# Moving DRAM copies earlier, operand sums later and weight sums apart in a one-core attention and MLP kernel

## The chip, the cores and the metric

The kernel runs on one core of a Trainium2 chip. The metric is the device time of one execution in microseconds (us). The engines are TensorE (PE, with its weight loads PEld), VectorE (DVE), ScalarE (ACT), GpSimd (POOL) and SyncE (SP), which here only issues DMAs. ACT issues DMAs too.

## The reference

A block with adaptive layer norm: attention on the last 512 keys of a cache, then a gated MLP. All data are 32-bit floats; S = 2048 tokens, D = 576, 32 query heads and 16 key heads of 128, F = 4608.

```python
sa, ca, ga, sb, cb, gb = (silu(c) @ w_mod).reshape(6, 576)
h = layernorm(x) * (1 + ca) + sa
p = softmax(q(h) @ k[-512:].T * 128 ** -0.5)         # per head
x = x + ga * ((p @ v[-512:]) @ wo)
h = layernorm(x) * (1 + cb) + sb
gate, up = h @ W_gate, h @ W_up
x = x + gb * ((gate * (gate > 0) * up) @ W_down)
```

## The kernel before, in words

Every product is made of 32-bit parts: an operand is split into `hi` (a rounded copy, made by ACT) and `lo` (the rest, a subtraction on POOL), and PE multiplies hi by hi, hi by lo and lo by hi.

Attention is 128 units, u = 0 to 127: one query head with 512 tokens. The instructions of PE, DVE, ACT and POOL are issued in the order in which the program is written. `step(name, t, fn)` puts extra work at the place t, in tenths of a unit: t = 705 is in the middle of unit 70. Each unit has one transposing reduction on DVE at line 474, by which units can be counted. SyncE's order is made by a scheduler, which may put a DMA that waits for nothing earlier than its step.

The extra work in the units:
- weights for the next heads are loaded (`rwA` for queries, `rkv` for keys and values, `roga` for the output), split and partly stored again;
- the MLP's gate and up weights are copied within DRAM into another layout, `wlay` and `wlay0` (`lay_steps`: 20 first copies, 68 big ones of shape 2x128x256, 64 small ones of shape 8 or 9x32x128), all on SyncE's queue;
- `w_later` makes the seven weight operands of feature pair 0 from `wlay0`, with loads (`wa_P`, `wb_P`), sums on POOL and stores;
- from H = 1070 on (unit 107), the second layer norm and the operands of the MLP's first token half.

The MLP uses a scheme of seven products (P1, P6, P2, P7, P5, P4, P3, in this order) in place of eight for a 2x2 block of tokens and features. One feature pair m is 256 features; m = 0 to 17 works on the first half of the tokens, m = 18 to 35 on the second. Seven token operands (B11, B21, B22, T1 to T4) stay in SBUF through a half. They are made from four quarters of h, `h0[j, k, t]` (t = 0, 1, 2 are the thirds along D), in place: `t3` overwrites (1,1) by (1,1) - (0,1), `t2` then adds (0,0), `t1` and `t4` come last. `h0_hi` makes `hi` on ACT, `h0_cut` makes `lo` on POOL, and most are stored and loaded again (`h_back`).

For m = 1 to 17 the weight operands are made while m - 1 is computed: four raw tiles `wr` (00, 01, 10, 11) are loaded from `wlay`, DVE makes four sums of them in place, and `w_split` splits each of the seven operands. For m = 18 to 35 they come back from DRAM. The down product of m - 1 is eight pieces `md`, spread over the products of m; each piece uses the one bank of `psW`, which is free again when DVE has added it to `acc` (line 594). A piece needs `hhi` and `hlo`, the split of the gated result, which `evac` makes: three DVE instructions (L969 to L971), `hi` on ACT, `lo` on POOL. `wd_prep` loads the two down-weight tiles of an m, multiplies them by the gate row on DVE (`rogb`, L221) and splits them. DVE's L967, once in each m, counts the m's.

Of the kernel before, what the change touches and what calls it, by code (L numbers as in the profile page):

```python
# [33 lines left out]
def kernel(  # L34
# [667 lines left out]
    def w_split(n, raw):  # L702
        w = w_tile(n)
        nc.scalar.copy(w[:, :, 0:3, :], raw)
# [8 lines left out]
    loads = []  # L713

    def w_prep(n):
        w_prep1(n)
        while loads:
            w_load(*loads.pop(0))

    def w_prep1(n):  # L720
        m, s = divmod(n, 7)
        if m >= NB:
            return
        s = order(m)[s]
# [7 lines left out]
        if s == "P1":  # L732
            s1 = wraw[m, "s1"] = pp.tile([P, 2, 3, P], F32, tag="hi", name=f"ws1_{m}")
            nc.vector.tensor_tensor(flat(s1), flat(r[1, 0]), flat(r[1, 1]), op=ALU.add)  # L734
        if s == "P1":
            w_split(n, r[0, 0])
        elif s == "P6":
            nc.vector.tensor_tensor(flat(r[1, 0]), flat(r[0, 0]), flat(r[1, 0]), op=ALU.subtract)  # L738
            nc.vector.tensor_tensor(flat(r[0, 0]), flat(wraw[m, "s1"]), flat(r[0, 0]), op=ALU.subtract)  # L739
            w_split(n, r[0, 0])  # L740
        elif s == "P2":
            w_split(n, r[0, 1])
        elif s == "P7":
            nc.vector.tensor_tensor(flat(r[0, 1]), flat(r[0, 1]), flat(r[0, 0]), op=ALU.subtract)
            w_split(n, r[1, 0])
        elif s == "P5":
            w_split(n, wraw[m, "s1"])
        elif s == "P4":
            w_split(n, r[1, 1])
        else:  # L750
            w_split(n, r[0, 1])

# [70 lines left out]
    def h0_here(s):  # L823
        for t in range(3):
            h0_hi(s, H0_CUT[s], t)
        hs = hop[0, s] = [hy0[s, t] for t in range(3)]
        for t in (0, 1, 2):
            a = h0[(*H0_CUT[s], t)]
            if t < 2:
                hs.append(hp.tile([P, 512], F32R, tag="hT", name=f"hz0_{s}_{t}"))  # L830
                nc.gpsimd.tensor_sub(hs[-1], a, hs[t].bitcast(F32))
            else:
                nc.gpsimd.tensor_sub(hs[2][64:96], a[64:96], hs[2][64:96].bitcast(F32))

    def h0_cut(s, x, t):
        a, n = h0[(*x, t)], 96 if t == 2 else P
        hi = hy0[s, t]
        if t < 2:
            lo = hp.tile([P, 512], F32R, tag="hT", name=f"hz0_{s}_{t}")
            nc.gpsimd.tensor_sub(lo, a, hi.bitcast(F32))  # L840
            stores.append((hkeep[0, s, 3 + t], lo))
        else:
            nc.gpsimd.tensor_sub(hi[64:96], a[64:96], hi[64:96].bitcast(F32))
# [364 lines left out]
    step("m5.l", 936, m5_back)  # L1208
    step("gb", 949, setd(mods, "gb", lambda: gate_row(5)))

    step("T.ohi2", e, o_hi, NU - 2)
    step("T.olo2", e, o_lo, NU - 2)
    for k, lay in enumerate(lay_steps()):
        for i, ab in enumerate(lay):
            step("lay", (480, 600)[k] + 3.4 * i, lambda ab=ab: nc.sync.dma_start(*ab))
    mextra = {}

    def mat(m, s, fn, *args):
        mextra.setdefault((m, s), []).append((fn,))

    for m in range(NB):
        for f in range(2):
            for k, fn in enumerate(wd_prep(m, f)):
                mat(m, (k, 3 + (k > 0))[f] if m else 2 * f + k, fn)
    for i in range(4):
        m = 2 + 2 * i
        for at_, fn in zip(((m - 1, 5), (m, 0), (m, 1), (m, 5)), ln_half(2 + i // 2, i % 2)):
            mat(*at_, fn)
# [7 lines left out]
    LEAD = 3  # L1236
    def mlp_slots():
        todo = []
        for m in range(NB):
            md = [lambda k=k, qt=qt: md_piece(m - 1, k, qt) for k in range(2) for qt in range(4)] if m else []  # L1240
            for i, s in enumerate(order(m)):
                flush_stores()
                if s not in ("P2", "P3"):
                    new_pair(m, s)
                else:
                    pair[m, s], kind[m, s] = (x[m, {"P2": "P1", "P3": "P5"}[s]] for x in (pair, kind))
                prod(m, s, 7 * m + i, 0)
# [52 lines left out]
    for s in ("P1", "P2", "P4", "P7", "P5", "P6", "P3"):  # L1300
        for xx in range(2):
            for fn in w_later(s, xx, (xp, "xm", 640)):
                step("w.l", t, fn)
                t = after(t + 5)
            step("w.e", t + 3, flush_stores)
            t = after(t + 5)
    assert t < 930, t
    for key, t, at_ in [(("l", 0, 0), 2, 96), (("l", 1, 0), 2, 96), (("l", 1, 1), 2, 122), (("l", 0, 1), 2, 122),
# [162 lines left out]
```

## Time and profile before

| | |
|---|---|
| median of 3 runs | 3068.1 us (3067.82 to 3068.15) |
| profiled execution | 3069.0 us, of which span 3067.2 us |
| busy, share of the span | PE 95%, DVE 68%, ACT 45%, POOL 61% |
| granted clock, mean | 0.981 |
| data moved | 427.24 MB, mean 139 GB/s |

"Profiled execution" is one run under the profiler; the span goes from its first to its last instruction, and all times in rows are from the start of that span. In rows of stretches, the columns after the length are the busy us of each engine with the number of instructions, the clock that PE was granted, the mean busy share of the 16 DMA engines, and the GB/s moved. A row "A <- B: 10.0, 4, 3.0" says that A's engine stood idle 10.0 us in all before A until B was done, 4 times, at most 3.0 us.

### The profile page before, as it was taken

How to read it: one execution, taken by the hardware profiler on the slowest of the kernel's cores; microseconds unless marked ns; L12 is line 12 of the kernel's file. 1: busy time of each engine (PE TensorE's matmuls, PEld its weight loads, DVE VectorE, ACT ScalarE, POOL GpSimd, SP SyncE). 2: the span in 40 equal slices, each digit the busy share in tenths (PEclk: the TensorE clock that was granted, in tenths of full speed). 3: DMA queues.
4: the chain of work that ended last, by engine and by line, in shares of the span. 5: the costliest groups of instructions: out<-in, count | busy, mean ns of one | idle time of the engine just before them, and what ended most of it. 6: DMA issues, size and time to landing. Idle time of an engine off the chain costs nothing. (4 is left out here: it accounts for less than half of the span.)

```text
span 3067.2 us, 41142 instructions
## 1 busy us (share of the span) xinstructions
PE 2914.7 (95%) x15406; PEld 2536.8 (83%) x15406; DVE 2092.0 (68%) x2909; ACT 1368.0 (45%) x1869; POOL 1874.8 (61%) x1315
## 2 busy tenths in 40 slices
PE   6799999999999779999988999999999999999999
PEld 5688888888888668888877788888888888888888
DVE  7878788888887558777877566666666544444444
ACT  5466676666666446666645433333333111111110
POOL 5578888888888568767776566667787311111111
PEclk9899999999999889999999999999999999999999
DMA  4011122112222223432244355667777944444543
GB/s 144 21 50 57 45 76 69 64 53 76 88 84 85 85 80 129 156 98 90 68 146 143 104 202 215 240 243 263 272 259 253 344 172 160 159 161 167 175 161 115
DMA packets 168679, 427.24 MB, mean 139 GB/s; under 512 B 15584, under 2 KB 62432, under 8 KB 168480
## 3 DMA queue, kind: packets, MB, share of 16 engines
q1 hardware_dynamic: 132848, 294.08, 29.4%
q10 hardware_dynamic: 35632, 130.53, 11.1%
q8 instruction: 122, 2.00, 0.3%
q14 instruction: 77, 0.63, 0.1%
HBM read 279.42 MB, written 173.44 MB: 148 GB/s over the span
## 5 line engine op out<-in xcount | busy, mean ns | idle before, releaser
L538 POOL TENSOR_TENSOR lo<-p,hi 128x1024 fp32r<-128x1024 f32 x256 | 612.9, 2416 | 1.1 <-ACT hi L518 0.8
L547 POOL TENSOR_TENSOR ks<-ks,p 128x512 f32<-128x512 f32 x256 | 339.6, 1326 | 295.7 <-ACT p L531 236.7
L594 DVE TENSOR_TENSOR acc<-md,acc 128x576 f32<-128x576 f32 x288 | 217.9, 756 | 437.8 <-PE md L583 437.8
L583 PE MATMUL md<-wogb,hhi 128*128 128x288 f32 x2304 | 472.1, 297 | 21.0 <-DVE acc L594 21.0
L583 PEld LDWEIGHTS md<-wogb,hhi 128*128 128x128 f32 x2304 | 386.6, 189 | 49.4 <-DVE acc L594 27.8
L459 DVE TRANSPOSE_TENSOR_REDUCE t<-s 128x32 f32<-128x1024 f32 x256 | 316.7, 1244 | 155.2 <-PE s L456 143.8
L946 PE MATMUL gu<-hop_T,wop 128*128 128x512 f32 (+1 forms) x1512 | 380.7, 395 | 3.0 <-DVE rb L564 3.0
L946 PE MATMUL gu<-hop_B,wop 128*128 128x512 f32 (+1 forms) x1512 | 379.1, 394 | 2.2 <-DMA wop<-wk_P 2.0
L583 PE MATMUL md<-wogb,hlo 128*128 128x288 f32 x1152 | 342.7, 297 | 12.0 <-POOL hlo L962 12.0
L382 PE MATMUL qps<-hTa,wA 128*128 128x512 f32 x1288 | 314.5, 396 | 15.1 <-ACT lfa L364 7.8
L946 PEld LDWEIGHTS gu<-hop_B,wop 128*128 128x128 f32 (+1 forms) x1512 | 279.1, 189 | 57.4 <-DMA wop<-wk_P 2.4
L962 POOL TENSOR_TENSOR hlo<-r,hhi 128x512 fp32r<-128x512 f32 x72 | 101.5, 1410 | 366.6 <-issue 244.7
L946 PEld LDWEIGHTS gu<-hop_T,wop 128*128 128x128 f32 (+1 forms) x1512 | 279.7, 190 | 55.0 <-DVE rb L564 3.1
L583 PE MATMUL wo<-woga,ohi 128*128 128x288 f32 x1472 | 311.6, 305 | 7.1 <-ACT wo L616 5.2
L382 PEld LDWEIGHTS qps<-hTa,wA 128*128 128x128 f32 x1288 | 245.8, 191 | 68.6 <-ACT lfa L364 8.2
L529 DVE TENSOR_TENSOR p<-s,mb 128x1024 f32<-128x1024 f32 x246 | 290.2, 1218 | 4.2
L518 ACT CAST hi<-p 128x1024 fp32r<-128x1024 f32 x256 | 269.1, 1051 | 7.2
L531 ACT ACTIVATE p<-p 128x1024 f32<-128x1024 f32 x246 | 259.8, 1056 | 7.9 <-DVE p L529 5.9
L583 PEld LDWEIGHTS wo<-woga,ohi 128*128 128x128 f32 x1472 | 243.1, 192 | 15.3 <-ACT wo L616 5.6
L583 PEld LDWEIGHTS md<-wogb,hlo 128*128 128x128 f32 x1152 | 217.7, 189 | 15.0 <-POOL hlo L962 15.0
L583 PE MATMUL wo<-woga,olo 128*128 128x288 f32 x736 | 220.2, 299 | 8.3 <-POOL olo L572 8.1
L434 ACT ACTIVATE qhi<-qps 128x512 fp32r<-128x512 f32 x128 | 76.4, 597 | 333.9 <-PE qps L382 333.6
(207 smaller groups left out, 6000.2 us busy)
## 6 DMA issues: line engine op xcount, KB each, us to landing
wop<-wk_P SPq DMA_DIRECT2D x133, 640.0 KB
wk_P<-wop ACTq DMA_DIRECT2D x119, 640.0 KB
wr<-wlay SPq DMA_DIRECT2D x68, 384.0 KB
dk<-wogb ACTq DMA_DIRECT2D x36, 576.0 KB
wogb<-dk SPq DMA_DIRECT2D x36, 576.0 KB
againq<-akq SPq DMA_DIRECT2D x18, 640.0 KB
rogb<-wd SPq DMA_DIRECT2D x36, 288.0 KB
rwA<-wq SPq DMA_DIRECT2D x32, 320.0 KB
```

Of the source, the lines that this page charges most:

```text
L382: return [lambda i=i, a=a, b=b: nc.tensor.matmul(ps, a, b, start=(i == 0), stop=(i == n - 1)) for i, (a, b) in enumerate(ops)]
L434: nc.scalar.activation(qhi[u], qst[u][0], AF.Copy, bias=0.0, scale=SCALE)
L459: nc.vector.tensor_reduce(t4[u][:, 2 * h:2 * h + 2, :].rearrange("p k b -> p (k b)"), t.rearrange("p k (b j) -> p (k b) j", j=32), axis=AX ...
L518: nc.scalar.copy(hi_[u, h], pt[u, h])
L529: nc.vector.tensor_tensor(p, t, bc[u][:, None, :].to_broadcast([P, 2, 512]), op=ALU.subtract)
L531: nc.scalar.activation(p, p, AF.Exp, bias=0.0, scale=1.0)
L538: nc.gpsimd.tensor_sub(lo_[u, h], pt[u, h], hi_[u, h].bitcast(F32))
L547: nc.gpsimd.tensor_tensor(ks_[u], ks_[u], p[:, j, :], op=ALU.add)
L583: nc.tensor.matmul(ps[:, half, :H2], a[:, sl], w[b][:, cs], start=(n == 0 and seed is None), stop=(n == 5), skip_group_check=seed is not None)
L594: nc.vector.tensor_tensor(av, ps[:, :, :H2], av, op=ALU.add)
L946: nc.tensor.matmul(ps, a, c, start=s not in ("P2", "P3") and i == 0, stop=i == len(ops) - 1, skip_group_check=True)
L962: nc.gpsimd.tensor_sub(lo, r, hi.bitcast(F32))
```

## The change

1. The copies. First and other copies form one list that starts at step 400 with 3.5 between steps; before, the first ones started at 480 and the others at 600, 3.4 apart. `w_later` has 8 in place of 5 between its steps and more places to choose from; the saved row m5 comes back at 1046 and not at 936.
2. The token operands. Steps of `h0_comb` and `h0_cut` come later, so that a sum that overwrites a tile stands about ten steps behind the split that reads it. The split of the third tile (t = 2) moves from POOL to DVE. T2 stays in SBUF: it is neither stored nor loaded again.
3. The MLP's weights. The four sums per m are other ones (S3, S2, S1, S4 in this order) and stand in P4 and P3 of m - 1 and in P6 and P2 of m, one in each; before, P4 had one, P3 two, P6 the fourth. Splits use the tiles that this leaves. The loads of the next m stand behind P2, P7, P5 and P4, one each. The gates of the down weights stand in P6 and P7, pieces of the layer norm for the second half two or three products later. The down pieces: one at the end of P1, two in P6, then one in each; before, two in P1.

```diff
+        w_split(n, {"P1": r[0, 0], "P6": wraw.get((m, "s2")), "P2": r[0, 1], "P7": r[1, 0], "P5": r[0, 0],
+                    "P4": r[1, 1], "P3": r[0, 1]}[s])
+
+    def w_sums(m, s):
...
+        out, a, b, op = {"S3": (r[1, 0], r[0, 0], r[1, 0], ALU.subtract),
+                         "S2": (wraw.get((m, "s2")), r[1, 1], r[1, 0], ALU.subtract),
+                         "S1": (r[0, 0], wraw.get((m, "s2")), r[0, 0], ALU.add),
+                         "S4": (r[0, 1], r[0, 1], wraw.get((m, "s2")), ALU.subtract)}[s]
+        nc.vector.tensor_tensor(flat(out), flat(a), flat(b), op=op)
...
-            nc.gpsimd.tensor_sub(hi[64:96], a[64:96], hi[64:96].bitcast(F32))
+            nc.vector.tensor_sub(hi[64:96], a[64:96], hi[64:96].bitcast(F32))
...
-    for k, lay in enumerate(lay_steps()):
-        for i, ab in enumerate(lay):
-            step("lay", (480, 600)[k] + 3.4 * i, lambda ab=ab: nc.sync.dma_start(*ab))
+    for i, ab in enumerate(sum(lay_steps(), [])):
+        step("lay", 400 + 3.5 * i, lambda ab=ab: nc.sync.dma_start(*ab))
...
+    def sums(m, i):
+
+        for k, s in {1: [(0, "S1")], 2: [(0, "S4")], 5: [(1, "S3")], 6: [(1, "S2")]}.get(i, []):
+            if 0 < m + k < NFP:
+                w_sums(m + k, s)
+        for fn in mextra.pop((m, i - 1, True), []):
+            fn()
+
+    def others(m, i):
+        w_prep(7 * m + i + 2)
+        for fn in mextra.pop((m, i - 1, False), []):
+            fn()
+        for ij in {2: [(1, 0)], 3: [(0, 0)], 4: [(1, 1)], 5: [(0, 1)]}.get(i, []):
+            if m + 1 < NFP:
+                w_load(m + 1, *ij)
...
                 prod(m, s, 7 * m + i, 0)
-                if m:
+                if m or i:
+                    sums(m, i)
+                    others(m, i)
+                if m and i:
                     md.pop(0)()
...
                 prod(m, s, 7 * m + i, 1)
                 wop.pop(7 * m + i)
-                if m and not i:
+                if m and i < 2:
                     md.pop(0)()
...
-                        ("B21", 2, 111), ("B22", 0, 112), ("B22", 1, 121), ("t3", 0, 118), ("t3", 1, 128),
-                        ("T3", 0, 122), ("t2", 0, 128), ("T3", 1, 131), ("t2", 1, 138),
+                        ("B22", 0, 112), ("B21", 2, 122), ("B22", 1, 122), ("t3", 0, 128), ("T3", 0, 132),
+                        ("t3", 1, 138), ("T3", 1, 142), ("B22", 2, 142), ("t2", 0, 148), ("T2", 0, 152),
```

SyncE's queue at the place where the big copies become dense after the change (units 53 to 55), before:

```order
L1215 DMA wlay<-wg 2x128x256
L188 DMA rwA_7403<-wq 128x640
L862 DMA wa_P_0_7531<-wlay_329 128x384
L202 DMA rkv_1_7562<-kv 128x512
L1215 DMA wlay<-wu 2x128x256
L217 DMA roga_7683<-wo 128x576
L188 DMA rwA_7750<-wq 128x640
L862 DMA wa_P_1_7812<-wlay_329 128x384
L1215 DMA wlay<-wu 2x128x256
```

and after the change, the same place:

```order
L1196 DMA wlay<-wg 2x128x256
L188 DMA rwA_7425<-wq 128x640
L844 DMA wa_P_0_7553<-wlay_329 128x384
L1196 DMA wlay<-wu 2x128x256
L202 DMA rkv_1_7585<-kv 128x512
L1196 DMA wlay<-wu 2x128x256
L1196 DMA wlay<-wg 2x128x256 x2
L217 DMA roga_7709<-wo 128x576
L1196 DMA wlay<-wu 2x128x256
L188 DMA rwA_7777<-wq 128x640
```

Up to here both queues hold the same DMAs, with one copy between the loads of one or two heads' weights; from here on the new one has two to three copies per unit, in the old one that begins 30 rows further on, at unit 70.

DVE at the end of unit 118 and the start of unit 119, before (`lfb_1_2` is the first third of quarter (1,1), L814 is the sum `t3`):

```order
L544 TENSOR_TENSOR ks118_15708<-p118_0_15693 128x512
L564 TENSOR_TENSOR rb117_15704<-pv117_15686,rb117_15704 128x512
L594 TENSOR_TENSOR acc14_139<-wo115_2_15725,acc14_139 128x576
L814 TENSOR_TENSOR lfb_1_2_15509<-lfb_1_2_15509,lfb_1_0_15374 128x512
L459 TENSOR_REDUCE t4_119_15756<-s119_0_15749 128x32
```

After the change, the same sum (L797) a unit later, at the end of unit 119:

```order
L544 TENSOR_TENSOR ks119_15837<-p119_0_15825 128x512
L564 TENSOR_TENSOR rb118_15833<-pv118_15815,rb118_15833 128x512
L819 TENSOR_TENSOR hy0_B21_2_15786<-h0_102_15439,hy0_B21_2_15786 32x512
L797 TENSOR_TENSOR lfb_1_2_15503<-lfb_1_2_15503,lfb_1_0_15370 128x512
L459 TENSOR_REDUCE t4_120_15894<-s120_0_15887 128x32
```

POOL's split that reads the old value stands in unit 118 in both; in the version after:

```order
L572 TENSOR_TENSOR olo116_15609<-rb116_15566,ohi116_15607 128x512
L547 TENSOR_TENSOR ks118_15701<-ks118_15701,p118_1_15694 128x512 x2
L817 TENSOR_TENSOR hz0_B22_0_15711<-lfb_1_2_15503,hy0_B22_0_15657 128x512
L538 TENSOR_TENSOR lo118_0_15741<-p118_0_15688,hi118_0_15691 128x1024
L538 TENSOR_TENSOR lo118_1_15743<-p118_1_15694,hi118_1_15739 128x1024
```

So the sum moved from the unit of its split to the one behind it, and a split of a third tile (L819) is new on DVE.

DVE from product P4 of m = 6 to P1 of m = 7, before (`ws1_7` and `wr7` are sums for m = 7, `rogb` is a gate, `r6` and `q6` are evacuations):

```order
L734 TENSOR_TENSOR ws1_7_19187<-wr7_10_19004,wr7_11_19100 128x768
L221 TENSOR_TENSOR rogb_13_19147<-rogb_13_19147,mrow5_12684 128x576
L969 TENSOR_TENSOR r6_19114<-gu39_19165,r6_19114 128x512
L970 TENSOR_TENSOR gu39_19165<-gu39_19165,r6_19114 128x512
L971 SCALAR_TENSOR_TENSOR r6_19114<-r6_19114,gu39_19165 128x512
L594 TENSOR_TENSOR acc7_132<-md5_1_3_19224,acc7_132 128x576
L738 TENSOR_TENSOR wr7_10_19004<-wr7_00_19002,wr7_10_19004 128x768
L739 TENSOR_TENSOR wr7_00_19002<-ws1_7_19187,wr7_00_19002 128x768
L969 TENSOR_TENSOR q6_18972<-gu38_19119,q6_18972 128x512
```

and after the change:

```order
L734 TENSOR_TENSOR wr7_10_19020<-wr7_00_19071,wr7_10_19020 128x768
L594 TENSOR_TENSOR acc6_131<-md5_1_2_19189,acc6_131 128x576
L951 TENSOR_TENSOR r6_19094<-gu39_19153,r6_19094 128x512
L952 TENSOR_TENSOR gu39_19153<-gu39_19153,r6_19094 128x512
L953 SCALAR_TENSOR_TENSOR r6_19094<-r6_19094,gu39_19153 128x512
L734 TENSOR_TENSOR ws2_7_19226<-wr7_11_19120,wr7_10_19020 128x768
L594 TENSOR_TENSOR acc7_132<-md5_1_3_19234,acc7_132 128x576
L951 TENSOR_TENSOR q6_18944<-gu37_19098,q6_18944 128x512
```

The gate has left P4, P3 has one sum in place of two, and the first needs tiles 00 and 10 where it needed 10 and 11.

More of the change, by code (lines that the diff above doesn't have):

```diff
@@ L724, in w_prep1 @@
         s = order(m)[s]
-        if m + 1 < NFP:
-            for ij in {"P7": ((0, 0), (1, 0)), "P4": ((1, 1),), "P3": ((0, 1),)}.get(s, ()):
-                loads.append((m + 1, *ij))
         if m % NFP == 0 or m >= NFP:
@@ L731, in w_prep1 @@
         r = {ij: wraw.get((m, *ij)) for ij in RAW}
[L732 to L751, printed above, removed]
+        w_split(n, {"P1": r[0, 0], "P6": wraw.get((m, "s2")), "P2": r[0, 1], "P7": r[1, 0], "P5": r[0, 0],
+                    "P4": r[1, 1], "P3": r[0, 1]}[s])
+    def w_sums(m, s):
+        r = {ij: wraw.get((m, *ij)) for ij in RAW}
+        if s == "S2":
+            wraw[m, "s2"] = pp.tile([P, 2, 3, P], F32, tag="hi", name=f"ws2_{m}")
+        out, a, b, op = {"S3": (r[1, 0], r[0, 0], r[1, 0], ALU.subtract),
[3 more added lines that the diff above has]
+        nc.vector.tensor_tensor(flat(out), flat(a), flat(b), op=op)
     TERMS = {"B11": "+00", "B21": "+10", "T2": "+11-01+00", "T3": "+11-01", "T1": "+01-00",
@@ L825, in h0_here, with h0_cut @@
             h0_hi(s, H0_CUT[s], t)
[L826 to L835, printed above, removed]
+        for t in range(3):
+            h0_cut(s, H0_CUT[s], t, True)
+    def h0_cut(s, x, t, stay=False):
         a, n = h0[(*x, t)], 96 if t == 2 else P
@@ L838, in h0_cut @@
         if t < 2:
-            lo = hp.tile([P, 512], F32R, tag="hT", name=f"hz0_{s}_{t}")
+            lo = hy0[s, 3 + t] = hp.tile([P, 512], F32R, tag="hT", name=f"hz0_{s}_{t}")
             nc.gpsimd.tensor_sub(lo, a, hi.bitcast(F32))
+        else:
+            nc.vector.tensor_sub(hi[64:96], a[64:96], hi[64:96].bitcast(F32))
+        if stay:
+            if t == 2:
+                hop[0, s] = [hy0[s, k] for k in range(5)]
+            return
+        if t < 2:
             stores.append((hkeep[0, s, 3 + t], lo))
-        else:
-            nc.gpsimd.tensor_sub(hi[64:96], a[64:96], hi[64:96].bitcast(F32))
         stores.append((hkeep[0, s, t], hi[:n]))
@@ L1223 @@
             for k, fn in enumerate(wd_prep(m, f)):
-                mat(m, (k, 3 + (k > 0))[f] if m else 2 * f + k, fn)
+                if m >= NFP:
+                    at_ = m, 3 * f
+                elif f and m:
+                    at_ = ((m - 1, 5), (m, 0), (m, 1))[k]
+                else:
+                    at_ = m, k + (k > 0 and m > 0) + 2 * f
+                mat(*at_, fn, sums=k == 1)
     for i in range(4):
         m = 2 + 2 * i
-        for at_, fn in zip(((m - 1, 5), (m, 0), (m, 1), (m, 5)), ln_half(2 + i // 2, i % 2)):
-            mat(*at_, fn)
+        for at_, fn in zip(((m - 1, 5), (m, 2), (m, 3), (m, 4)), ln_half(2 + i // 2, i % 2)):
+            mat(*at_, fn, sums=at_ == (m - 1, 5))
     later = {s: [fn for t in range(3) for fn in h_later(1, s, t)] for s in TERMS}
@@ L1247, in mlp_slots @@
                 prod(m, s, 7 * m + i, 0)
-                if m:
+                if m or i:
+                    sums(m, i)
+                    others(m, i)
+                if m and i:
                     md.pop(0)()
-                elif filler:
+                elif filler and not m:
                     filler.pop(0)()
-                for fn in todo:
-                    fn()
                 prod(m, s, 7 * m + i, 1)
                 wop.pop(7 * m + i)
-                if m and not i:
+                if m and i < 2:
                     md.pop(0)()
-                elif filler:
+                elif filler and not i:
                     filler.pop(0)()
@@ L1292, in then @@
         return go
-    calm = [10 * u + k for u in range(54, 96) for k in ((6, 9) if u % 2 else (0, 4, 6, 9))]
+    calm = [10 * u + k for u in range(54, 107) for k in ((6, 9) if u % 2 else (0, 4, 6, 9))]
     def after(t):
@@ L1303 @@
                 step("w.l", t, fn)
[L1304 to L1307, printed above, removed]
+                t = after(t + 8)
+            step("w.e", t, flush_stores)
+    assert t < 1040, t
     for key, t, at_ in [(("l", 0, 0), 2, 96), (("l", 1, 0), 2, 96), (("l", 1, 1), 2, 122), (("l", 0, 1), 2, 122),
[6 rows of a table removed]
[6 rows of a table added]
         if key[0] == "l":
@@ L1320 @@
             step("h0.h", H + at_, h0_hi, key, H0_CUT[key], t)
-            step("h0.c", H + at_ + (4 if at_ // 10 % 2 else 6), then(lambda key=key, t=t: h0_cut(key, H0_CUT[key], t)))
-    step("h0.e", H + 181, flush_stores, 0, nc.sync)
-    for t, s in ((1236, "B11"), (1256, "T2"), (1257, "B21"), (1266, "T3")):
+            step("h0.c", H + at_ + (6 if t == 2 else 4 if at_ // 10 % 2 else 6),
+                 then(lambda key=key, t=t: h0_cut(key, H0_CUT[key], t, key == "T2")))
+    step("h0.e", H + 172, flush_stores, 0, nc.sync)
+    for t, s in ((1251, "B11"), (1257, "B21"), (1266, "T3")):
         step("h.l", t, h_back, 0, s)
```

16 lines of the change are left out of this document (4 added, 12 removed), and 8 rows, old and new, of the table t.

## The prediction

> **What bounds it now.** I read the timeline in stretches first: busy time and granted clock of each engine, between times that I took from the DVE's one L474 per attention unit and its one L967 per feature pair m of the MLP. Then, for each stretch that is too long, the waits, and last the rows of the engine that was waited for.
>
> Busy time by stretch (times are us from the span's start):
>
> ```profile
> core 0: us, PE busy (x) PEld busy (x) DVE busy (x) ACT busy (x) POOL busy (x), PEclk, DMA share, GB/s
> 184.20:915.60 731.40, 728.56 (x3862) 633.95 (x3861) 604.03 (x881) 499.17 (x672) 619.01 (x381) 1.00 0.21 66
> 977.50:1152.50 175.00, 136.29 (x645) 116.64 (x644) 100.66 (x146) 83.51 (x112) 109.23 (x72) 0.87 0.25 84
> 1152.50:1469.80 317.30, 315.78 (x1666) 274.36 (x1665) 250.52 (x378) 205.39 (x271) 239.40 (x147) 1.00 0.35 116
> 1571.80:1671.90 100.10, 82.44 (x395) 70.41 (x393) 76.27 (x98) 49.89 (x68) 69.32 (x42) 0.90 0.38 125
> 1780.50:2431.66 651.16, 618.35 (x3339) 539.47 (x3338) 417.27 (x478) 210.11 (x299) 439.84 (x388) 0.99 0.71 254
> 2431.66:3031.42 599.76, 599.76 (x3299) 530.91 (x3298) 274.02 (x357) 69.45 (x102) 88.24 (x68) 1.00 0.50 168
> ```
>
> The same stretches, counting only L474 (three rows: attention units) and only L967 (two rows: m's):
>
> ```profile
> 184.20:915.60 731.40, 42.23 (x60) 1.00 0.21 66
> 977.50:1152.50 175.00, 7.04 (x10) 0.87 0.25 84
> 1571.80:1671.90 100.10, 4.22 (x6) 0.90 0.38 125
> ...
> 1780.50:2431.66 651.16, 11.72 (x17) 0.99 0.71 254
> 2431.66:3031.42 599.76, 11.75 (x17) 1.00 0.50 168
> ```
>
> TensorE is the bound where nothing disturbs it: a unit takes 731.40/60 = 12.19 us and an m of the second half of the MLP 599.76/17 = 35.28 us, both with PE busy throughout. Three stretches fall behind this. Stage A, 977 to 1152: 175.0 for 10 units, 53 us lost. Stage B, 1572 to 1672: 100.1 for 6 units, 27 us lost. Stage C, the first half of the MLP: 651.16/17 = 38.30 us per m, 3.02 us lost on each of 17, 51 us in all. The change touches all three, so each has its own term.
>
> **Stage A, the copies.** SyncE's queue there and earlier, then the DMA issues from 923 to 1143.2 and the throughput of that window in 40 slices, then the longest waits of 978 to 1153:
>
> ```profile
> 781.29 0.58 SPq L1215 DMA_DIRECT2D wlay<-wg  x1
> ...
> 1013.25 5.25 SPq L188 DMA_DIRECT2D rwA<-wq  x1
> 1018.55 0.58 SPq L1215 DMA_DIRECT2D wlay<-wu  x1
> 1019.17 13.04 SPq L1215 DMA_DIRECT2D wlay<-wg  x2
> 1032.32 5.67 SPq L202 DMA_DIRECT2D rkv<-kv  x1
> ```
>
> ```profile
> GB/s 147 60 83 74 69 93 100 50 90 48 98 101 132 49 158 48 51 100 168 78 48 93 48 164 49 48 80 90 48 51 150 48 50 88 72 54 77 96 48 48
> ...
> wlay<-wu SPq DMA_DIRECT2D x19, 256.0 KB
> wlay<-wg SPq DMA_DIRECT2D x18, 256.0 KB
> ```
>
> ```profile
> DVE roga L221 <- DMA roga<-wo: 29.4, 5, 9.3
> POOL wa_P L872 <- DMA wb_P<-wlay: 27.6, 5, 9.6
> ```
>
> A copy or a load that SyncE issued in 0.3 to 0.6 us at 781 blocks it for 5 to 6 us at 1013 to 1032, and the weights that stand behind the copies (wo here) arrive late. When copies run alone the queue moves 48 GB/s, its floor in the slices. 37 big copies take 220.2 us with the loads between them: 5.95 us each. Their steps stand 3.4 apart, 0.34 units, 4.14 us. So each copy leaves the queue 1.81 us behind, 67 us over 37; 53 were lost, and about 14 went into the loads' lead.
>
> The change takes nothing off a copy. By the order of instructions the dense part only begins sooner, after 43 copies instead of 51, so 45 big copies stand in it and not 37. They are 3.5 apart, 4.27 us: 1.68 us behind each, 76 us, less the same 14 of lead: 62 against 53. I take +10. The ends: +23 if no lead is left to take, and -53 if the earlier place hides all of it. I stay near the upper end because the stage from 184 to 915 has PE as full (728.56 of 731.40) and the same loads between the copies as the later one: no unit there is cheaper to delay. The 64 small copies of the last columns move too. I cost them at nothing: they are issued between loads after 1152.50, where PE is full (315.78 of 317.30 us). Their cover is the slack of the queue there; if it is gone, they too cost up to the big ones' excess, 1.68 us each.
>
> The Trainium skill ("DMA: Bandwidth & Descriptors", section on why a DMA increments its semaphore by 16) says that a copy is spread over the largest number of engines, up to 16, that divides the slowest dimension, always the lowest-numbered ones; for 2x128x256 that is two. By the page's 27 GiB/s per engine I would estimate 4.5 us per copy, 45 of them would lag by only 10 us and the total would be some 50 us lower than mine; the 5.95 us measured decides here.
>
> w_later's steps go from 5 to 8 apart, the saved row m5 comes back 110 steps later: the same instructions in units where PE is full, nothing either way.
>
> **Stage B, the MLP operands.** Longest wait of PE, then DVE's operand sums (L814) in the timeline and all of them as a group:
>
> ```profile
> PE qm L482 <- DVE t L474: 17.4, 4, 6.6
> ```
>
> ```profile
> 1602.21 4.52 DVE L814 TENSOR_TENSOR lfb<-lfb,lfb 128x512 f32<-128x512 f32 x2 [4.37 <-POOL hz_B L840]
> ...
> 1636.56 0.69 DVE L814 TENSOR_TENSOR h<-h,h 96x512 f32<-96x512 f32 x1 [5.69 <-POOL hy_B L843]
> ```
>
> ```profile
> L814 DVE TENSOR_TENSOR lfb<-lfb,lfb x8: 683/1798/2857, 1584.3 to 1666.1; 128x512 f32<-128x512 f32 x8
> ```
>
> A sum overwrites a tile that POOL's split still has to read. That split stands behind POOL's row sums of the same unit, so DVE stands still, the next unit's maxima behind the sum are late, and PE waits for them (4 times, up to 6.6 us). After the change each sum stands a whole unit, 12.2 us, behind its split, more than any wait here (5.69), so I count these waits gone. What stays is the sums' own time on DVE, 0.68 to 2.86 us each, and seven short splits of the third tiles, new on DVE, in the same range. DVE is busy 76.27 of 100.1 us; at full pace the same work fills 73 us, so it has 2 us free per unit if one sum is in it. Six of the units hold one sum, one split or both, and one has three sums and runs over by 2 to 5 us. I leave 7 of the 27 us: -20. The ends are 0 (all 19 operations at 2.86, 54 us on an engine with about 20 free) and -27. T2's five stores and five loads go away on a queue that nobody waits for there: nothing.
>
> **Stage C, the weight sums.** The waits of the stage, a piece of DVE's timeline at the turn from one m to the next with PE's wait that follows, and the sums as groups:
>
> ```profile
> PE md L583 <- DVE acc L594: 19.2, 15, 2.8
> PE md L583 <- POOL hlo L962: 11.7, 12, 2.8
> ```
>
> ```profile
> 1795.04 2.53 DVE L221 TENSOR_TENSOR rogb<-rogb,mrow 128x576 f32<-128x576 f32 x1
> 1797.49 0.68 DVE L969 TENSOR_TENSOR r<-gu,r 128x512 f32<-128x512 f32 x1
> ...
> 1800.21 0.95 DVE L738 TENSOR_TENSOR wr<-wr,wr 128x768 f32<-128x768 f32 x1
> 1801.29 1.82 DVE L739 TENSOR_TENSOR wr<-ws,wr 128x768 f32<-128x768 f32 x1
> ...
> 1807.12 0.75 DVE L594 TENSOR_TENSOR acc<-md,acc 128x576 f32<-128x576 f32 x1
> ```
>
> ```profile
> 1807.92 0.54 PE L583 MATMUL md<-wogb,hhi 128*128 128x288 f32 x2 [2.75 <-DVE acc L594]
> ```
>
> ```profile
> L221 DVE TENSOR_TENSOR rogb<-rogb,mrow 128x576 f32<-128x576 f32 x33 | 51.0, 1547 | 0.0
> L739 DVE TENSOR_TENSOR wr<-ws,wr 128x768 f32<-128x768 f32 x16 | 26.5, 1655 | 2.1
> ```
>
> A product lasts 35.28/7 = 5.0 us; an m is 14 half products and 8 down pieces, 35.28/22 = 1.6 us each. In two of them DVE has 4 to 5 us of extra work: a weight sum and the gate of the down weights ahead of P4's evacuation (L969, started only when the gate ended), and two sums ahead of P3's. So the second down piece waits for DVE's sum of the first (2.75 us), and hlo comes late. These two waits are 30.9 us of the 51; the rest is clock (0.99) and gaps too short to be listed. The change keeps four sums per m but puts one into each of P4, P3, P6 and P2 (1.66 us each), moves the gates to P6 and P7 (1.55), and starts the down pieces half a product later, one behind P1 and two in P6. The tightest place is P6: the sum of piece A, weight sum, gate and sum of piece B are 0.75 + 1.66 + 1.55 + 0.75 = 4.7 us, and PE comes back for the bank after about 4.8 (three of these blocks): it just fits, and a sum or a gate at its longest (2.53) costs 1 us. hlo gains 1.6 us of slack and loses the gate ahead of it. The four loads of the next m are still four, one behind each of P2, P7, P5 and P4 on SyncE's queue (rival 4 is what that could cost); the layer norm's halves move by two or three products in four of the m's, the same instructions in places with as much room: nothing. I take the 30.9 and 8 of the rest: 36.0 us per m, -39. The ends are -51 (all PE-bound) and +17, an m of 39.3 that holds one more wait like the 1 us above.
>
> **The sum.** The profiled execution took 3069.0 us (span 3067.2), 0.9 above the median of the runs. 3069.0 + 10 - 20 - 39 = 3020, as a median 3019 us.
>
> **Rivals.** (1) Stage C trades its waits for new ones: in P6 as counted, or hlo behind the splits on POOL, which is busy 439.84 of 651.16 us. Two thirds of the waits come back: -12 instead of -39, 3046 us.
> (2) Stage B keeps its loss, because the seven splits and the sums on DVE find POOL in the way: 3039 us. For it speaks that a sum takes 0.68 us at best and 1.80 in the median. The Trainium skill ("SBUF — State Buffer", section on who interferes with whom) has a rule for it: a VectorE instruction with two SBUF inputs contends with a GpSimd instruction that reads SBUF, and the one that comes second waits out the whole instruction. The spread of the group agrees; it does not say how many of the new ones meet POOL.
> (3) The copies are hidden in their earlier place: 3069 - 53 - 20 - 39 = 2957, as a median 2956. Against it stands the 48 GB/s floor.
> (4) Slower: P4's weight sum waits for its load. In the new queue order wr_00 stands behind wr_11, whose buffer is free only when P4's split is done, one product before the sum. DVE executes in order, so a late wr_00 holds the sum of the down piece and P4's evacuation. This decides from an m of 39.2 us, 3.9 above the bound; one full product of delay, 5.0 us per m, gives 40.3, stage C +34 and 3092 us. Against it: the splits, which read the same loads, waited for them hardly at all:
>
> ```profile
> ACT wop L704 <- DMA wr<-wlay: 3.9, 2, 2.5
> ```
>
> **Chances.** My forecast 0.67 (its own range 3003 to 3035: +-13 on the copies, +-8 on stage C, +-5 on stage B), rival 1 0.15, rival 2 0.07, rival 3 0.06, rival 4 0.05. The range reaches over rivals 1 and 2 and over part of the copies' better end: 2995 to 3052. A difference under 0.2%, 6 us, can hardly be told from none here. Rivals 1 to 3 and the forecast are all faster by more: faster 0.92 with a little taken off for two of them together, same 0.03, slower 0.05.
>
> **What will show it.** Stage A: SyncE blocked for 5 to 6 us at each issue from about 760 to 1010 instead of 960 to 1140, some 16 units in which 60 us are lost, and units at 12.1 us around 1000 to 1150 of the old count. Stage B: no L797 behind POOL's L817, the six units at 12 to 14 us. Stage C: an L949 every 36 us, the wait of md for acc under 5 us in all. The forecast is wrong if the copies' stage loses 30 us more or less than 62, or if an m stays above 37.

## The result, and the profile after

The changed kernel took 3032.2 us (median of 4 runs, 3032.1 to 3034.3) against 3068.1: a ratio of 0.9884, 95% interval 0.9867 to 0.9901. The profiled span is 3030.4 us where it was 3067.2. It is faster by 36 us where 49 were forecast, and inside the range.

The two executions are compared at the same marks, the starts of L474 (attention units) and of the first evacuation of P2 in each m (L967 before, L949 after). The numbers are us:

| stretch | before | after | difference | forecast |
|---|---|---|---|---|
| start to unit 57 | 781.0 | 782.4 | +1.4 | 0 |
| units 57 to 83 (stage A, old and new place) | 372.0 | 382.4 | +10.4 | +10 |
| units 83 to 116 | 406.3 | 405.0 | -1.3 | 0 |
| units 116 to 124 (stage B) | 124.8 | 102.2 | -22.6 | -20 |
| unit 124 to m = 0 | 51.9 | 50.9 | -1.0 | 0 |
| m = 0 | 44.6 | 40.3 | -4.3 | 0 |
| m = 1 to 17 (stage C) | 651.2 | 631.6 | -19.5 | -39 |
| second token half | 635.6 | 635.6 | 0 | 0 |

Stages A and B came out as forecast; stage C gave half. The stretches of the profile after, to be read like those of before:

```profile
core 0: us, PE busy (x) PEld busy (x) DVE busy (x) ACT busy (x) POOL busy (x), PEclk, DMA share, GB/s
184.20:781.90 597.70, 596.18 (x3164) 519.58 (x3163) 491.10 (x723) 406.61 (x546) 500.08 (x301) 1.00 0.19 64
781.90:1018.95 237.05, 189.32 (x898) 161.45 (x897) 141.41 (x201) 117.04 (x160) 151.84 (x103) 0.89 0.27 93
1018.95:1569.30 550.35, 549.31 (x2918) 478.37 (x2917) 446.10 (x674) 362.04 (x483) 438.93 (x279) 1.00 0.30 97
1582.20:1657.60 75.40, 75.10 (x395) 64.46 (x393) 68.75 (x98) 49.81 (x68) 62.84 (x37) 1.00 0.44 143
1763.00:2394.70 631.70, 613.59 (x3340) 535.51 (x3339) 446.43 (x478) 208.75 (x298) 428.23 (x387) 0.99 0.72 260
2394.70:2994.45 599.75, 599.75 (x3300) 531.03 (x3299) 272.55 (x357) 69.45 (x102) 87.99 (x68) 1.00 0.49 171
```

And how many units (L474, first two rows) and m's (L949, last row) three of them hold:

```profile
781.90:1018.95 237.05, 9.86 (x14) 0.89 0.27 93
1582.20:1657.60 75.40, 4.22 (x6) 1.00 0.44 143
...
1763.00:2394.70 631.70, 11.63 (x17) 0.99 0.72 260
```

The second row of the stretches is the new stage A: 237.05 us for 14 units, 67.9 more than 14 x 12.08, the median unit. Before and behind it PE is full. The fourth is the old stage B, six units in 75.40 us instead of 100.10. The fifth is stage C, 37.16 us per m. SyncE's queue in the new stage A looks as it did in the old one, many a copy, or a load behind copies, taking 5 to 6 us:

```profile
953.58 5.34 SPq L1196 DMA_DIRECT2D wlay<-wu  x1
959.02 5.25 SPq L188 DMA_DIRECT2D rwA<-wq  x1
964.32 6.13 SPq L1196 DMA_DIRECT2D wlay<-wg  x2
970.49 6.04 SPq L1196 DMA_DIRECT2D wlay<-wu  x1
976.63 6.71 SPq L202 DMA_DIRECT2D rkv<-kv  x1
```

In units 116 to 124 PE's wait for the maxima (17.4 us before) has nearly gone. The sums themselves are still dear: 1.47 us in the mean for the eight of full size, where they took 2.04 before and 0.68 at best. PE's wait after the change, then the sums before and after (the numbers behind the count are busy us, mean ns of one, and us that DVE stood idle just before them):

```profile
PE qm L482 <- DVE t L474: 1.5, 1, 1.5
```

```profile
L814 DVE TENSOR_TENSOR lfb<-lfb,lfb 128x512 f32<-128x512 f32 x8 | 16.2, 2043 | 7.2 <-POOL hz_B L840 7.2
L797 DVE TENSOR_TENSOR lfb<-lfb,lfb 128x512 f32<-128x512 f32 x8 | 11.6, 1469 | 0.1
```

In stage C PE's list of waits holds one line of weight, and 13.5 of its 17.8 us stand at the second down piece of P6, 2.7 in P2 and 1.7 in P4. The wait for hlo (11.7 us) is gone, that for DVE's sum of the down piece (19.2) is not:

```profile
PE md L583 <- DVE acc L594: 17.8, 15, 3.1
```

DVE's weight sums there, by form (S3, S2, S1 and S4 in this order are `wr<-wr,wr`, `ws<-wr,wr`, `wr<-ws,wr`, `wr<-wr,ws`), took 135.3 us; the four groups of before took 97.8 us (L739's 26.5 and the three that stand first here, ahead of the four of after):

```profile
L744 DVE TENSOR_TENSOR wr<-wr,wr 128x768 f32<-128x768 f32 x16 | 25.1, 1571 | 0.4 <-POOL wop L706 0.4
L738 DVE TENSOR_TENSOR wr<-wr,wr 128x768 f32<-128x768 f32 x16 | 24.9, 1555 | 0.0
L734 DVE TENSOR_TENSOR ws<-wr,wr 128x768 f32<-128x768 f32 x16 | 21.3, 1330 | 0.0
...
L734 DVE TENSOR_TENSOR wr<-wr,ws 128x768 f32<-128x768 f32 x16 | 44.8, 2803 | 0.0
L734 DVE TENSOR_TENSOR wr<-ws,wr 128x768 f32<-128x768 f32 x16 | 36.0, 2247 | 0.0
L734 DVE TENSOR_TENSOR wr<-wr,wr 128x768 f32<-128x768 f32 x16 | 29.6, 1847 | 0.0
L734 DVE TENSOR_TENSOR ws<-wr,wr 128x768 f32<-128x768 f32 x16 | 24.9, 1556 | 0.0
```

The longest of PE's waits, in the P6 at 2117 us, first DVE, then PE:

```profile
2116.80 0.76 DVE L594 TENSOR_TENSOR acc<-md,acc 128x576 f32<-128x576 f32 x1 [2.61 <-PE md L583]
2117.48 2.81 DVE L734 TENSOR_TENSOR wr<-ws,wr 128x768 f32<-128x768 f32 x1
2120.21 3.74 DVE L221 TENSOR_TENSOR rogb<-rogb,mrow 128x576 f32<-128x576 f32 x1
2123.88 0.74 DVE L594 TENSOR_TENSOR acc<-md,acc 128x576 f32<-128x576 f32 x1
```

```profile
2124.67 0.53 PE L583 MATMUL md<-wogb,hhi 128*128 128x288 f32 x2 [3.11 <-DVE acc L594]
```

A sum and a gate, which take 0.95 and 0.75 us at best, take 2.81 and 3.74, and the second down piece of P6 waits 3.11 us. Why they last so long is seen at 2050, POOL first, then DVE:

```profile
2050.51 0.74 POOL L705 TENSOR_TENSOR wop<-wr,wop 32x256 fp32r<-32x256 f32 x1 [1.34 <-ACT wop L704]
2051.21 1.28 POOL L706 TENSOR_TENSOR wop<-wr,wop 128x512 fp32r<-128x512 f32 x1
2052.46 1.42 POOL L181 TENSOR_TENSOR wogb<-rogb,wogb 128x576 fp32r<-128x576 f32 x1
2053.84 1.27 POOL L768 TENSOR_TENSOR hx_T<-hx_T 128x512 f32<-128x512 f32 x1
```

```profile
2050.94 5.00 DVE L734 TENSOR_TENSOR wr<-wr,ws 128x768 f32<-128x768 f32 x1
2055.86 0.74 DVE L594 TENSOR_TENSOR acc<-md,acc 128x576 f32<-128x576 f32 x1
```

POOL runs four instructions without a gap and ends at 2055.11; DVE's sum, begun inside the first, ends at 2055.94, 0.83 us behind the last. That fits a sum that did nearly all of its 0.95 us of work when POOL had stopped. Most sums that last long end so, or in a pause of POOL, but not all: the one of 2218.71 lasts 4.86 us and ends while POOL's L706, begun without a pause, is running, which then takes 1.98 us in place of 1.28. Of the 97 sums and gates of stage C 53 last longer than at best; four of them end inside a run in which the trace shows no pause. DVE's instructions that take one input from PSUM show nothing of this over the whole of stage C; the first row (minimum, median and maximum in ns) is one of these, the second is the gate, with both inputs in SBUF:

```profile
L953 DVE SCALAR_TENSOR_TENSOR r<-r,gu x34: 686/687/692, 1763.8 to 2375.3; 128x512 f32<-128x512 f32 x34
...
L221 DVE TENSOR_TENSOR rogb<-rogb,mrow x33: 745/752/3765, 1764.5 to 2360.7; 128x576 f32<-128x576 f32 x33
```

The Trainium skill ("SBUF — State Buffer", section "Who interferes with whom") says that a VectorE instruction with two SBUF inputs contends with a GpSimd instruction that reads SBUF, that the ports they share are an exclusive lock, and that the order of issue decides who blocks. The trace agrees on who contends; it shows that the loser here waited for four instructions in a row and not for one.

So the theory for stage C was: the sums and gates on DVE wait out POOL's chain, and the chains are longest from m = 5 on, where POOL makes the operands of the second token half (L768, L778) as well. PE's first wait of the stage is at 1967.9 us, in m = 7. The rivals were late loads and a DVE that is simply full.

### The profile page after: what moved, and what is told of

It is laid out like the page before. It is cut to its first block, busy times and chain, and to the rows that moved or that the text cites. A ratio compares the mean times of both kernels' runs of the same rounds, so it can differ in the third digit from the quotient of the medians.

```text
span 3030.4 us, 41167 instructions
## 1 busy us (share of the span) xinstructions
PE 2901.1 (96%) x15406; PEld 2527.0 (83%) x15406; DVE 2116.5 (70%) x2916; ACT 1365.2 (45%) x1869; POOL 1857.3 (61%) x1308
## 4 chain that ended last, share of the span: by engine, by line
PE 83%; DVE 7%; DMA 4%; POOL 2%; issue 2%; ACT 2%; SPq 0%; ACTq 0%; POOLq 0%; DVEq 0%
PE gu L928 25%; PE md L583 14%; PE wo L583 12%; PE qps L382 11%; PE s L455 3%; PE s L456 3%; PE s L454 3%; PE pv L558 3%; PE pv L557 3%; PE pv L556 3%; DVE wr L734 1%; DMA roga<-wo 1%; DMA rkv<-kv 1%; PE qm L482 1%; DVE rogb L221 1%
## 5 line engine op out<-in xcount | busy, mean ns | idle before, releaser
L583 PE MATMUL md<-wogb,hhi 128*128 128x288 f32 x2304 | 472.4, 297 | 17.8 <-DVE acc L594 17.8
L928 PE MATMUL gu<-hop_B,wop 128*128 128x512 f32 (+1 forms) x1512 | 372.5, 393 | 0.0
L382 PE MATMUL qps<-hTa,wA 128*128 128x512 f32 x1288 | 314.8, 396 | 21.5 <-DVE rb L564 11.7
L944 POOL TENSOR_TENSOR hlo<-r,hhi 128x512 fp32r<-128x512 f32 x72 | 94.2, 1309 | 382.9 <-issue 240.9
L928 PE MATMUL gu<-hop_T,wop 128*128 128x512 f32 (+1 forms) x1260 | 313.2, 392 | 3.0 <-DVE rb L564 3.0
L928 PEld LDWEIGHTS gu<-hop_T,wop 128*128 128x128 f32 (+1 forms) x1260 | 231.2, 188 | 46.6 <-DVE rb L564 3.1
L943 ACT CAST hhi<-r 128x512 fp32r<-128x512 f32 x72 | 44.7, 621 | 462.0 <-DVE r L953 458.7
```

Of the source, the lines that this page charges most:

```text
L382: return [lambda i=i, a=a, b=b: nc.tensor.matmul(ps, a, b, start=(i == 0), stop=(i == n - 1)) for i, (a, b) in enumerate(ops)]
L583: nc.tensor.matmul(ps[:, half, :H2], a[:, sl], w[b][:, cs], start=(n == 0 and seed is None), stop=(n == 5), skip_group_check=seed is not None)
L928: nc.tensor.matmul(ps, a, c, start=s not in ("P2", "P3") and i == 0, stop=i == len(ops) - 1, skip_group_check=True)
L944: nc.gpsimd.tensor_sub(lo, r, hi.bitcast(F32))
```

## Experiments

Each kernel is the changed kernel with the edit shown, if nothing else is said. Ratios are to the kernel before. Stretches are between the marks of the table above.

**The copies, back at their old steps.**

```diff
-    for i, ab in enumerate(sum(lay_steps(), [])):
-        step("lay", 400 + 3.5 * i, lambda ab=ab: nc.sync.dma_start(*ab))
+    for k, lay in enumerate(lay_steps()):
+        for i, ab in enumerate(lay):
+            step("lay", (480, 600)[k] + 3.4 * i, lambda ab=ab: nc.sync.dma_start(*ab))
```

> The changed kernel with only the copies' steps put back (20 first copies from step 480, the others from step 600, 3.4 apart); all else stays changed. My theory: the big copies cost SyncE's queue the same wherever they stand, and their dense stretch was 10.4 us dearer because it holds more copies (from attention unit 57 to 83 the two profiles took 372.0 and 382.4 us). Expected 3022 us (3017 to 3026), stage A with about 53 us lost at units 73 to 83 again. Rival: the other moves in these units (the weight operands' steps 8 apart, the saved row's later return) cost the 10 us: then 3032, no change.

Measured: ratio 0.9855 (0.9841 to 0.9870), 3026.7 us beside 3070.4 for the kernel before, just above the expected range, since stage C took 635.4 us in this run, 3.8 more, though nothing was changed there. Units 57 to 83 took 371.5 us, 10.9 less than in the changed kernel and as many as before. So the copies' part cost its 10 us, and the other moves in these units cost nothing that shows.

**The copies with 128 rows as the slowest dimension.**

```diff
-        step("lay", 400 + 3.5 * i, lambda ab=ab: nc.sync.dma_start(*ab))
+        step("lay", 400 + 3.5 * i,
+             lambda ab=ab: nc.sync.dma_start(*[x.rearrange("f p n -> p f n") for x in ab]))
```

> The changed kernel with every copy's axes reordered so that the slowest dimension is 128 or 32 (128x2x256 in place of 2x128x256): the same bytes to the same places. Theory: 2x128x256 is carried by two of the 16 DMA engines, which is why a copy takes 5.4 us and blocks the queue; with 128 rows it is spread over all and takes under 1 us. The stall at units 57 to 70 (68 us) goes. The scheduler puts these copies, now short, all at the program's start, 28 MB in all, so that the first heads' weights come late: up to 100 us lost there. Expected 2965 to 3065 in all, with units 57 to 70 at 12.1 us each. Rival: 48 GB/s is what this queue moves for a copy within DRAM whatever its shape; then 28 MB take 580 us, ahead of the loads of the first units, and the total is above 3300.

Measured: ratio 0.9689 (0.9667 to 0.9711), 2975.2 us. Units 57 to 83 took 317.1 us, 65.3 less. All copies went out between 34 and 217 us, a big one in about 0.65 us of the queue:

```profile
50.57 1.28 SPq L1196 DMA_DIRECT2D wlay<-wg  x2
51.89 1.28 SPq L1196 DMA_DIRECT2D wlay<-wu  x2
```

Unit 4 began at 148.1 us instead of 138.2: the start paid 10 us for them. The rival, a rate that belongs to copies within DRAM whatever their shape, is out.

**The same copies, issued by ACT.** As above, with `nc.scalar.dma_start`.

> The same reordered copies, but issued by ACT, whose order is that of the program, so that each stands at its step (400 + 3.5 i). Theory of the two DMA engines: no copy blocks a queue, 152 issues of 0.33 to 0.40 us on ACT over 540 us are hidden (ACT is 45% busy), the 68 us lost at units 57 to 70 go: 2964 us (2958 to 2972). Rival, the rate of a copy within DRAM does not depend on its shape: ACT is blocked for about 5 us by each of the 68 big copies, in every third of a unit, and the time is over 3100.

Measured: ratio 0.9657 (0.9641 to 0.9673), 2965.3 us, as forecast. Units 57 to 83 took 317.1 us again, and unit 4 began at 137.2. Two rows of stretches follow: in the changed kernel 7 us in which SyncE's queue moves only copies, and here 740 to 1019 us, which takes in all of the changed kernel's stage A:

```profile
1000.00:1007.00 7.00, 2.16 (x12) 1.50 (x11) 1.18 (x3) 3.37 (x5) 4.61 (x4) 1.00 0.14 49
```

```profile
740.00:1019.00 279.00, 277.41 (x1465) 240.50 (x1465) 230.52 (x329) 192.74 (x263) 246.55 (x161) 1.00 0.38 116
```

With 2x128x256 the 16 DMA engines are busy to 0.14, little over two sixteenths, at 49 GB/s. With 128x2x256 PE is full throughout at 116 GB/s, and a copy lands 3.2 us after its issue in the median:

```profile
wlay<-wu ACTq DMA_DIRECT2D x12, 256.0 KB, 3.2
```

This is the rule of the Trainium skill that the prediction named ("DMA: Bandwidth & Descriptors", section on why a DMA increments its semaphore by 16): as many engines, up to 16, as divide the slowest dimension. The runs agree with it. The rate per engine that the Trainium skill gives on the same page, from which the prediction estimated a lag of only 10 us for 45 copies, did not hold, as the prediction had it: in the changed kernel the 45 big copies from 738.75 to 1007.56 us left the queue at 5.97 us each.

**The same edit on the kernel before.** `nc.scalar` and the reordered axes, at the old steps.

> The kernel before with one edit: its copies reordered (128 rows slowest) and issued by ACT at their old steps. Theory: stage A's 53 us go and nothing else moves: 3068 - 54 = 3014 us (3009 to 3020), so that this edit alone is worth more than the whole change. Rival: in the old place the loads of the weight operands stand right behind the copies that they read and hold SyncE's queue: 3025 or more.

Measured: ratio 0.9836 (0.9821 to 0.9851), 3018.2 us; units 57 to 83 took 319.6 us instead of 372.0. This one edit is worth more than the whole change (0.9884, 0.9867 to 0.9901). It touches neither stage B (124.1 us) nor stage C (650.8).

**Stage B: the old steps.** The new table of steps for `h0_hi`, `h0_cut` and `h0_comb` replaced by the old one.

> The changed kernel with the old table of steps for the token operands (each sum 4 to 7 steps behind the split that reads its tile); the third tiles' splits stay on DVE and T2 stays in SBUF. Theory: the sums wait for POOL's splits again, PE for the maxima: stage B (units 116 to 124) back from 102.2 to about 125 us, 3055 us (3048 to 3060). Rival: the splits on DVE and the stores and loads of T2 that are gone made the gain; then 3030 to 3036.

Measured: ratio 0.9957 (0.9942 to 0.9971), 3055.5 us; units 116 to 124 took 122.4 us, 20.2 more. The wait is back:

```profile
PE qm L482 <- DVE t L474: 18.6, 5, 6.3
```

**Stage B: the third tiles' splits back on POOL.**

```diff
-            nc.vector.tensor_sub(hi[64:96], a[64:96], hi[64:96].bitcast(F32))
+            nc.gpsimd.tensor_sub(hi[64:96], a[64:96], hi[64:96].bitcast(F32))
```

> The changed kernel with the seven splits of the third tiles (t = 2) of the token operands back on POOL instead of DVE; the later steps and the kept T2 stay. Theory: stage B's 22.6 us came from the distance between split and sum alone, so the six units from 117 stay at 12 to 14 us: 3030 to 3036 us. Rival: moving the splits off POOL is what let POOL keep up; then half or more of the 22.6 us come back, 3043 or more.

Measured: ratio 0.9915 (0.9900 to 0.9930), 3042.2 us, more than expected. Units 116 to 124 took 106.3 us, 4.1 more, and the turn to the MLP (unit 124 to the end of m = 0) 94.6 instead of 91.2. PE waits for POOL now:

```profile
PE pv L558 <- POOL lo L538: 2.4, 5, 0.7
```

So the distance between split and sum made about 20 of stage B's 22.6 us (by the run with the old steps), and the splits' move to DVE some 4, and up to 3.4 behind stage B: it helped, where the prediction's second rival had it do harm. That T2 stays in SBUF was not tested by itself.

**Stage C without POOL's work for the second half.** The sums in `comb` and both remainders in `cut` of `h_later` are left out; the second half's output is another one.

> The changed kernel without POOL's part of the second token half's operands: the 21 sums (L768), 14 remainders (L778) and 7 short ones are left out, so the output of the second half is not the reference's; all loads, ACT's copies and stores stay. Theory: in stage C a weight sum or a gate on DVE (two inputs in SBUF) lasts until POOL's back-to-back instructions are done, up to 5 us, and from m = 5 on POOL's chains are longer by this work; without it the sums stay under 3 us as in m = 1 to 4, PE's waits for acc (17.8 us) fall below 4, stage C is 612 to 618 us instead of 631.6, and the kernel 3012 to 3020 us. Rival: the waits come from late loads or from the DMA engines, 0.72 busy there: unchanged, 3028 to 3034.

Measured: ratio 0.9805 (0.9789 to 0.9822), 3008.4 us. Stage C took 608.7 us, 22.9 less, even more than expected, and PE's waits in it are gone. The weight sums took 110.4 us in place of 135.3, the gates 31.9 in place of 45.2:

```profile
PE md L583 <- DVE acc L594: 0.5, 2, 0.3
```

```profile
1765.44:2374.12 608.68, 607.49 (x3338) 533.34 (x3336) 410.00 (x478) 207.84 (x298) 368.81 (x345) 1.00 0.75 270
```

All loads were still made (DMA share 0.75, it was 0.72), so late loads are out, and DVE ran as many instructions (478), so a DVE that is simply full is out too. PE was also busy 6.1 us less with as many matmuls (613.59 to 607.49), beside a granted clock of 0.99 with the pauses and 1.00 without: part of what the pauses cost seems to be paid in slower matmuls.

**Stage C: S1 one product earlier**, in P1, so that P6 has only the gate.

```diff
-        for k, s in {1: [(0, "S1")], 2: [(0, "S4")], ...
+        for k, s in {0: [(0, "S1")], 2: [(0, "S4")], ...
```

> The changed kernel with one weight sum of the MLP (S1) moved from P6 to P1, one product earlier, where DVE has no evacuation; the gate stays in P6. Theory: of the 17.9 us that PE waits for DVE's sums of the down pieces in stage C, 13.5 stand at the second piece of P6, because S1 (2.25 us in the mean) and the gate (1.4 to 3.8) stand between two pieces there. They go: 3032 - 13 = 3019 us (3015 to 3024). Rival: DVE is late in the whole m, and the waits come back in P1 and P2: 3029 to 3035.

Measured: ratio 0.9857 (0.9841 to 0.9873), 3026.6 us; stage C 628.0 us, 3.6 less where 13 were expected, and within what profiles of the unchanged MLP code differ by (626.7 to 635.4 us). The waits moved. PE still waited 12.8 us for `acc`, the longest time in P4, where S3 met a chain of seven instructions on POOL:

```profile
PE md L583 <- DVE acc L594: 12.8, 8, 4.6
```

```profile
2254.61 1.28 POOL L706 TENSOR_TENSOR wop<-wr,wop 128x512 fp32r<-128x512 f32 x1
...
2261.65 1.25 POOL L778 TENSOR_TENSOR hx_T<-hx_T,hy_T 128x512 fp32r<-128x512 f32 x1
```

```profile
2255.47 8.25 DVE L734 TENSOR_TENSOR wr<-wr,wr 128x768 f32<-128x768 f32 x1
```

**Stage C: the second half's work spread.** Layer norm in m = 2 to 5, the 63 pieces at five per m from m = 4, in P7, P5 and P1.

```diff
-        m = 2 + 2 * i
+        m = 2 + i
...
+        mat(4 + i // 5, (2, 3, 3, 6, 6)[i % 5], fn)
```

> The changed kernel with the second half's operand work spread: its layer norm in m = 2 to 5 instead of 2, 4, 6, 8, and its 63 pieces at five per m from m = 4 to 16, in the products P7, P5 and P1, where DVE has no weight sum (P7 has a gate); before, three per m in 5 to 8 and one in each product in 9 to 16. Nothing is left out. Theory (a DVE instruction with two SBUF inputs waits out POOL's chain): with POOL's extra work away from the sums, PE's waits for acc fall by half or more, stage C by 8 to 18 us: 3014 to 3024 us. Rival: it is POOL's total, 26 us per m, that counts, not its place: 3029 to 3035.

Measured: ratio 0.9892 (0.9877 to 0.9907), 3033.3 us; stage C 633.4 us: no gain, as the rival had it. The wait for `acc` fell from 17.8 to 6.7 us, as the theory says, but splits came late instead:

```profile
PE md L583 <- DVE acc L594: 6.7, 7, 2.8
PE gu L928 <- POOL wop L706: 6.5, 4, 2.0
PE gu L928 <- DVE q L953: 2.3, 1, 2.3
```

**Copies on ACT and the pieces of m = 9 to 16 elsewhere**: in P7, P7, P5, P5, P4, P4, P3; then with S1 in P1 and the pieces in P2, P7, P7, P5, P5, P5, P4.

```diff
-        mat(9 + i // 7, i % 7, fn)
+        mat(9 + i // 7, (2, 2, 3, 3, 4, 4, 5)[i % 7], fn)     # second: (1, 2, 2, 3, 3, 3, 4), S1 in P1
```

> The changed kernel with the reordered copies on ACT, and in m = 9 to 16 the seven pieces of the second half's operands in P7, P7, P5, P5, P4, P4, P3 instead of one in each product, so that P6 and P2 hold none. Theory: POOL's chain in P6, where DVE has a sum and a gate between two down pieces, gets shorter, PE's waits at P6 go (13.5 of 17.9 us in the changed kernel): 2952 to 2960 us. Rival: the chains in P7 to P3 get longer by as much, splits come late and PE waits for them, as in the spread version (6.5 us): 2962 to 2970 us.

> As the version before, but S1 in P1 and the pieces in P2, P7, P7, P5, P5, P5, P4, so that P1 and P6 hold none. Theory: 2948 to 2958 us, since neither the sum in P1 nor the gate in P6 meets POOL's extra work. Rival: three pieces in P5 make POOL's chain there 4 us long and the splits behind it late: 2960 to 2970 us.

Measured: ratios 0.9744 (0.9727 to 0.9760) and 0.9776 (0.9761 to 0.9791), 2990.2 and 2999.8 us, with stage C at 653.0 and 664.4: both slower than the copies alone, and more than the rivals had. POOL does the same work in all these versions, so its place counts and not only its total. In the second PE waits least for DVE's sums of the down pieces, and for POOL's splits instead:

```profile
PE gu L928 <- POOL wop L706: 32.9, 12, 8.1
...
PE md L583 <- DVE acc L594: 2.2, 2, 1.8
```

POOL runs its instructions in the order of the program, and each product's split has a date there. Two or three pieces ahead of a split delayed it by more than the sums gained.

**The best version: copies on ACT, S1 in P1.**

> The changed kernel with the reordered copies on ACT and the weight sum S1 in P1. The two gains, 66 us in stage A and 3.6 us in stage C, are in different stages and add: 2962 us (2956 to 2968). Rival: they don't add, because S1's 3.6 us lay inside what stage C differs by from one build to the next (626.7 to 635.4 us in four profiles of the same code): then 2965 as with the copies alone.

Measured: ratio 0.9648 (0.9633 to 0.9662), 2961.0 us: faster than both kernels. Units 57 to 83 took 317.1 us, stage C 628.3. Against the copies alone (0.9657, 0.9641 to 0.9673) S1's share can't be told: stage C took between 626.7 and 635.4 us in the six profiles of the same code there (the changed kernel, the three runs on the copies that start from it and the two on stage B).

## Why the prediction came out as it did

- **Stage A, right: +10 forecast, +10.4 measured.** 45 copies instead of 37 in a dense stretch, each with the same excess, was the right account (5.97 us each after, 5.95 before); that nothing in the earlier place hides them was right too (rival 3 out). That the two agree within half a us is luck in part: the loss is 67.9 us where 62 were forecast. In the stage matmuls are also slower, 189.32 us for 898 or 0.211 us each, against 549.31 / 2918 = 0.188 behind it, at a clock of 0.89. That is 20 us of PE's time; how much of it adds to the loss, and how much only fills waits for the queue, is not shown.
- **Stage B, right: -20 forecast, -22.6 measured.** The cause, a sum that waits for the split of the tile it overwrites, is shown by the old steps alone (20.2 us back). The forecast put 7 us aside for three sums in one unit; 75.40 us for six units leave 2.9. The working that gave DVE 2 us free per unit does not come out of its own numbers, since 76.27 us of work do not fit into 73; there was room because the work itself got shorter, 68.75 us for the same 98 instructions.
- **Stage C, right in kind and half in size: -39 forecast, -19.5 measured.** The failed step is the price of one weight sum, "1.66 us each", and with it P6's 4.7 us that "just fits" into 4.8. The 64 sums took 2.11 us in the mean (135 / 64). In P6 S1 took 2.25 us in the mean and the gate behind it 1.89, at most 3.77, so the block is 5.6 us long; 0.8 us too much in 16 m's are 13 us in all, and PE waited 13.5 there, in ten of the m's. The prediction named P6 as the place and a sum at its longest as the danger, and 1 us as its cost; it took the mean that L739 had in the old places for the new ones, where POOL's runs beside the sums are others, and 2.53 us for the longest, although L738 took up to 3.88 in stage C of the profile before. Against the six profiles of 626.7 to 635.4 us the gain is 16 to 25 us, short of 39 in each. In rows: PE's idle time fell from 651.16 - 618.35 = 32.8 us to 18.1, so 14.7 of the 30.9 counted went, and its busy time by 4.8 of the 8.
- What made the price is POOL's work beside the new places, which the sum has no term for: without its 42 instructions on the second half's operands stage C is 22.9 us shorter again, 42.4 less than before, where 39 were forecast. The kernel before has these instructions too, and what it would gain without them was not tested. The layer norm's pieces, which moved and were costed at "nothing", were not tested alone either. An m above 37 (37.16) and a wait of md for acc above 5 us (17.8) are the signs that the prediction itself had named for being wrong there.
- **m = 0**, 4.3 us shorter, had no term; without it the total would lie that much further from the forecast, so this is luck. It holds the first sums for m = 1, S3 and S2. The cause is not shown: with the copies alone the kernel before took 41.9 us there, and the changed MLP code 38.7 to 41.5 in its profiles.
- Rival 1 (stage C trades its waits, 3046 us) described what happened, in P6 as it said, but not by hlo; the outcome lies between it and the forecast. Rival 4 did not occur: DVE's list of waits in stage C names PE alone, no load.

## What to carry to other kernels

Read the shape of a DRAM copy before its place: a slowest dimension of 2 kept the 16 DMA engines busy to 0.14 only and cost 52 us in the old place and 65 in the new. An instruction with two SBUF inputs on DVE has no price of its own while POOL works; price it with up to the length of POOL's gapless run beside it, and count what else the change leaves on POOL. Work moved out of one DVE block's way on an in-order queue lands in front of something else there, so look at the next date on that queue before moving it.

## What the runs showed of the hardware

- A DVE sum with both inputs in SBUF (0.95 us at best) took 5.00 us beside four, and 8.25 us beside seven POOL instructions that ran without a gap, and ended 0.83 and 0.82 us behind the last. In these two cases it was not let in between two of them; elsewhere it sometimes was. 34 DVE instructions with one input in PSUM (L953) kept 0.69 us within 6 ns.
- A load of 128 rows issued behind 2x128x256 copies (959.02) blocked the issuing queue for 5.25 us, although the 16 DMA engines were busy to 0.14 only in a stretch of copies alone.
- In a stage with pauses the matmuls were slower too: 0.211 us each at a granted clock of 0.89, 0.188 at 1.00 behind it.
